# Decode attention with two key heads a unit in one TensorE loop, in place of one key head a unit

## The chip, the cores and the metric

The kernel runs on one core of one Trainium2 chip. The metric is the device time in microseconds of that core. "Before" takes 446.25 us, the median of three runs (446.05 to 446.79). Two numbers: the *time* of an execution, which is the metric, and its *span*, which is what the trace covers, from the first to the last instruction.

## The reference, cut to what matters

Two attention layers, A and B, decode one token for each of 4 batches. They differ in what they read of the key and value caches: A reads all 8192 positions, B the last 2048.

```python
B, Sq, D = 4, 1, 512
Hq, Hkv, Sk, Dh = 32, 8, 8192, 128              # rep = Hq // Hkv = 4
q = (x @ wq).reshape(B, Sq, Hq, Dh).transpose(0, 2, 1, 3)
k = repeat(k_cache, rep, axis=1)                # B: only [:, :, Sk - 2048:, :]
v = repeat(v_cache, rep, axis=1)
p = softmax(einsum("bhqd,bhkd->bhqk", q, k) * Dh ** -0.5)
o = einsum("bhqk,bhkd->bhqd", p, v)
y = o.transpose(0, 2, 1, 3).reshape(B, Sq, Hq * Dh) @ wo
# output: concatenate([y_A, y_B], axis=-1)      everything bf16
```

The kernel has to read 184.56 MB from HBM. A's two caches are 134 MB of it, B's 34 MB, the four weight matrices 17 MB.

## The kernel before: the parts that matter

The work is cut into 40 *units*. A unit of A is one key head of one batch: 2 MB of K and 2 MB of V, 128 partitions with 64 positions (16 KB) each. A unit of B is four heads. K and V have four slots each. For every unit TensorE transposes K (T), multiplies it with the queries to get the scores (S), and multiplies the exponentials of the scores with V (PV). DVE finds the maximum and subtracts it, ACT takes exp, DVE and POOL add up the probabilities. After all batches of a head, its outputs are multiplied with that head's rows of wo.

The order of the instructions of one unit on TensorE, and which unit's values it carries:

```python
TOKENS = [("T", 0), ("T", 1), ("OT",), ("T", 2), ("T", 3), ("S", 0), ("S", 1), ("X",),
          ("T", 4), ("T", 5), ("S", 2), ("S", 3), ("PV", 0), ("PV", 1), ("OL",),
          ("T", 6), ("T", 7), ("S", 4), ("S", 5), ("PV", 2), ("PV", 3), ("S", 6), ("S", 7), ("OPJ",)]

def pv_unit(u):                      # L is the last unit
    if u < L - 1:
        return u - 1
    return None if u == L - 1 else L - 2
```

The end is treated specially. The last K is loaded directly after the K before it, ahead of two V, and no values stand between the last K and its scores except those of unit L-2. The values of the last two units come after the scores of the last one, and the last V arrives in quarters. `pe_filler` issues matmuls whose results nobody uses, to keep TensorE busy between the quarters:

```python
add(dve_sub(L)); add(dve_sum(L)); add(dve_rcp(L))
add(act_exp(L))
add(pool_ar2(L))
for c in range(NQ):
    pe_PV(L - 1, c)
add(dve_norm(L - 1))
for c in range(NQ):
    pe_PV(L, c)
    if c < NQ - 1:
        pe_filler(2)
add(dve_norm(L))
pe_OPJ(L // Bn)
# ... (queue of loads, on SyncE)
for u in range(1, NU + 1):
    if u < L:
        sp_K(u)
        if u == L - 1:
            sp_K(L)                  # the last K, right after the one before it
    # ... then V of unit u - 1
# after the last V: the last 0.5 MB of wo in four pieces, then the stores
```

Of the kernel before, what the change touches and what calls it, by code (L numbers as in the profile page):

```python
# [6 lines left out]
BF16 = mybir.dt.bfloat16  # L7
# [7 lines left out]
def bass_concat_heads__gqa_block_cached__sliding_block_cached__decode_kernel(  # L15
# [21 lines left out]
    DC = D // 128  # L37
    NT = SK // 128
    SB = SK // W
    NQ = 4  # L40
    assert SB == 4 and HKV % SB == 0 and NT % 32 == 0 and REP == 4
    TQ = NT // NQ
    NB = NT // 8
    NCMAX = SB * REP
    assert NT * 2 * REP <= 512 and NCMAX <= 16 and Bn <= 8
# [4 lines left out]
    NKS, NVS, NKT, NPT = 4, 4, 4, 4  # L50
    NW = 64
    NR = 4
# [6 lines left out]
    units = []  # L59
    for gg in range(HKV // SB):  # L60
        for b in range(Bn):
            units.append(dict(P=1, b=b, S=2, J=NT // 2, CPT=2 * REP, hq0=gg * SB * REP, nhq=SB * REP, g0=gg * SB, gg=gg))
    NU_B = len(units)
    for g in range(HKV):
        for b in range(Bn):
            units.append(dict(P=0, b=b, S=1, J=NT, CPT=REP, hq0=g * REP, nhq=REP, g0=g))
    NU = len(units)
    L = NU - 1
    NG = NU // Bn
    NG_B = NU_B // Bn  # L70
    LB0, NLB = NU_B + 2, 4
    LB1 = LB0 + (L - 1 - LB0) // NLB * NLB
    assert NLB == Bn and NKS == NVS == NPT == NLB
    first_group = {1: 0, 0: NG_B}
    last_group = {1: NG_B - 1, 0: NG - 1}

    def kv_src(cache, u, q=None):
        un = units[u]
        if un["P"] == 0:
            ap = cache[un["b"], un["g0"]].rearrange("(p t) d -> p t d", p=128)  # L80
            return ap if q is None else ap[:, q * TQ:(q + 1) * TQ, :]
        base = cache[un["b"], un["g0"] + 2 * q, SK - W:SK, :]
        JB = NT // 2
        return bass.AP(tensor=base.tensor, offset=base.offset,
                       ap=[[JB * DH, 64], [SK * DH, 2], [1, JB * DH]])

    def kv_dst(buf, slot, u, q=None):
        un = units[u]
        if un["P"] == 1:
            JB = NT // 2  # L90
            return buf[:, slot, q * JB:(q + 1) * JB, :]
        if q is not None:
            return buf[:, slot, q * TQ:(q + 1) * TQ, :]
        return buf[:, slot, :, :]

    with ExitStack() as es:
# [5 lines left out]
        def ps(name):  # L102
            return es.enter_context(nc.psum_tensor(name, [128, 512], F32))
# [4 lines left out]
        K_sb = sb("K_sb", [128, NKS, NT, DH], BF16)  # L108
        V_sb = sb("V_sb", [128, NVS, NT, DH], BF16)
        KT_sb = sb("KT_sb", [128, NKT, 8 * 128], BF16)  # L110
        W1 = sb("W1", [128, HQ * D], BF16)
        W2 = sb("W2", [128, HQ * D // 2], BF16)
# [3 lines left out]
        NGQ = HQ // REP  # L116
        NGG = HKV // SB
        RQA = sb("RQA", [128, Bn, NGQ, 2, 2 * REP], BF16)
        RQB = sb("RQB", [128, Bn, NGG, 2, 2, 4 * REP], BF16)
        RQc = sb("RQc", [128, Bn, 2, 2 * REP], BF16)  # L120
        zt = sb("zt", [128, Bn], BF16)
        permE = sb("permE", [128, 2, 2, 64], BF16)
        MK = sb("MK", [128, 16], F32)
        MASKB = sb("MASKB", [128, 16], F32)
        M1m = sb("M1m", [128, 16], F32)
        MBm = sb("MBm", [128, 16], F32)
        x_sb = sb("xo_sb", [Bn, 2, D], BF16)
        xT = sb("xT", [128, 2, DC, Bn], BF16)
        QT = sb("QT", [128, 2, Bn, HQ], BF16)
        M1 = sb("M1", [128, 16], F32)  # L130
        MB = sb("MB", [128, 16], F32)
        L1 = sb("L1", [128, 16], F32)
        LB = sb("LB", [128, 16], F32)
        RL = sb("RL", [128, 4, 16], F32)
        Dt = sb("Dt", [128, NT * 2 * REP], F32)
        PT = sb("PT", [128, NPT, NT * 2 * REP + NW], BF16)

        def pt_cols(u, c0, n):
            return PT[:, u % NPT, c0:c0 + n]
        OTg = sb("OTg", [128, 16, Bn], BF16)  # L140
        ORx = sb("ORx", [64, REP, REP, 32], BF16)
        OL = sb("OL", [128, SB, REP, Bn], BF16)
        osb = x_sb
        oacc = sb("oacc", [Bn, D], F32)
        dummy = sb("dummy_t", [128, 2], F32)
        banks_f = [ps("ps%d" % i) for i in range(8)]
        sem_k = [sm("s_k%d" % i) for i in range(NKS)]
        sem_v = [sm("s_v%d" % i) for i in range(NVS)]
        sem_vl = [sm("s_vl%d" % i) for i in range(NQ)]
        sem_wl = [sm("s_wl%d" % i) for i in range(REP)]  # L150
        sem_x = [sm("s_x0"), sm("s_x1")]
        sem_w1 = [sm("s_w1_%d" % i) for i in range(NQP)]
        s_w2 = sm("s_w2")
        sem_out = [sm("s_out0"), sm("s_out1"), sm("s_out2")]
        s_T, s_S, s_PV, s_OPJ = sm("s_T"), sm("s_S"), sm("s_PV"), sm("s_OPJ")
        s_Ed, s_Ea = sm("s_Ed"), sm("s_Ea")
        s_max, s_sub, s_sum, s_rcp = sm("s_max"), sm("s_sub"), sm("s_sum"), sm("s_rcp")
        s_ocp, s_exp, s_otr = sm("s_ocp"), sm("s_exp"), sm("s_otr")
        s_ar1, s_ar2, s_setup = sm("s_ar1"), sm("s_ar2"), sm("s_setup")
        s_pm, s_pm2, s_mk = sm("s_pm"), sm("s_pm2"), sm("s_mk")  # L160
        s_acp = sm("s_acp")
        s_Eq, s_rq, s_opc = sm("s_Eq"), sm("s_rq"), sm("s_opc")
        s_mk0, s_perm = sm("s_mk0"), sm("s_perm")

        KTB = [0, 1, 2]
        STB = [3, 4]
        OTB = [5, 6]
        OPB = 7

        def bank_f(i):  # L170
            return banks_f[i]

        def bank_bf(i):
            return banks_f[i].bitcast(BF16)

        K_sbf = K_sb.bitcast(F32)
        W1wq = W1[:, :].rearrange("p (c n) -> p c n", c=DC)
        W1wo = W1[:, :].rearrange("p (g r n) -> p g r n", g=HKV, r=REP)
        W2wo = W2[:, :].rearrange("p (g r n) -> p g r n", g=SB, r=REP)

        def wo_of(gi):
            if gi == 0:
                return W2wo, 0
            if gi < NG_B:
                return W1wo, 0
            return W1wo, SB + (1 if gi == NG - 1 else 0)

        def sem_of(key):
            t = key[0]
            if t in ("K", "Kh"):  # L190
                return sem_k[key[1] % NKS]
            if t in ("V", "Vh"):
                return sem_v[key[1] % NVS]
            if t == "VL":
                return sem_vl[key[1]]
            if t == "WL":
                return sem_wl[key[1]]
            if t == "x":
                return sem_x[key[1]]
            if t == "out":  # L200
                return sem_out[key[1]]
            if t == "W1":
                return sem_w1[key[1]]
            if t == "wo":
                return sem_w1[2]
            if t == "pm":
                return s_pm if key[2] == 0 else s_pm2
            if t == "E":
                if jobs[key[1]]["kind"] in ("xT", "QP", "perm"):
                    return s_Eq  # L210
                return s_Ed if evac_eng[key[1]] == "dve" else s_Ea
            return {
                "W2": s_w2, "T": s_T, "S": s_S, "PV": s_PV, "OPJ": s_OPJ,
                "max": s_max, "sub": s_sub, "sum": s_sum, "rcp": s_rcp, "otr": s_otr,
                "ocp": s_ocp, "exp": s_exp, "ar1": s_ar1, "ar2": s_ar2, "setup": s_setup, "pset": s_setup,
                "mk": s_mk, "acp": s_acp, "mk0": s_mk0, "perm": s_perm, "rq": s_rq, "OPJc": s_opc,
            }[t]

        DMA_KEYS = ("K", "Kh", "V", "Vh", "VL", "WL", "x", "out", "W1", "W2", "wo", "mk")

        plan = {e: [] for e in ("sp", "pe", "act", "dve", "pool")}

        turn = [None]

        def op(eng, fn, waits=(), inc=None):
            plan[eng].append(dict(fn=fn, waits=[w for w in waits if w is not None], inc=inc, turn=turn[0]))
# [4 lines left out]
        jobs = []  # L231
        bank_last = {}
        evac_eng = {}
        tjob_idx = {}
        qp_idx = {}
        xt_idx = {}
        perm_idx = {}
        ol_idx = {}
        norm_key = {}
        ot_uses = []  # L240

        def new_job(kind, eng, **kw):
            idx = len(jobs)
            step = 2 if turn[0] is not None and kind in ("OT", "OL") else 1
            bank = (jobs[-1]["bank"] + step) % 3 if jobs else 0
            jobs.append(dict(kind=kind, idx=idx, bank=bank, prev=bank_last.get(bank), **kw))
            bank_last[bank] = idx
            evac_eng[idx] = eng
            return idx

        def bankfree(idx):
            return ("E", jobs[idx]["prev"]) if jobs[idx]["prev"] is not None else None

        def pe_job_xT(P):
            idx = new_job("xT", "dve", P=P)
            xt_idx[P] = idx
            bk = bank_bf(KTB[jobs[idx]["bank"]])

# [760 lines left out]
```

## Time and profile before

| before | value | where it is read |
|---|---|---|
| time, median | 446.25 us | run times |
| span of the profiled execution (its time: 447.8 us) | 446.1 us | page, first line |
| DMA busy | 9 tenths in 38 of 40 slices | page, part 2 |
| sum of packet durations | 440.1 us on each of 16 engines | added up from the trace's packet records |
| last big transfer ends | 440.65 us | packet records, on the time axis of the views |
| from there to the end | 5.4 us | 446.07 - 440.65 |

From the profile page: the span, the busy time of each engine with its share of the span and its instructions, then two rows of the part with 40 slices (busy tenths of the DMA engines, and GB/s), and the count of packets.

```profile
span 446.1 us, 14783 instructions
PE 348.1 (78%) x6789; PEld 317.0 (71%) x6789; DVE 195.2 (44%) x451; ACT 179.0 (40%) x202; POOL 42.0 (9%) x127
...
DMA  8999999999999999999999999999999999999993
GB/s 336 417 407 439 414 421 417 419 420 422 424 424 424 429 422 423 426 426 432 428 428 426 428 432 426 428 424 425 430 429 429 423 426 432 430 425 425 428 415 113
DMA packets 17318, 185.01 MB, mean 415 GB/s; under 512 B 1908, under 2 KB 2440, under 8 KB 4872
```

The DMA engines are the limit from the second slice to the last but one. TensorE has 78% and waits in between. The view of waits says for what (engine, tile, line, what was waited for, then us in total, number of waits, longest):

```profile
PE ps L351 <- DMA K_sb<-in_A_k_cache_dram: 20.2, 16, 2.6
PE ps L417 <- DMA V_sb<-in_A_v_cache_dram: 17.9, 13, 2.0
```

In the view of windows each row is a stretch of time with the busy us of every engine, then granted TensorE clock, DMA share and GB/s:

```profile
120.00:400.00 280.00, 227.24 (x4409) 207.17 (x4405) 121.66 (x281) 117.92 (x135) 25.73 (x82) 0.96 1.01 427
436.00:441.00 5.00, 4.37 (x127) 3.78 (x124) 1.69 (x6) 0.42 (x1) 0.80 (x2) 1.00 0.47 178
441.00:446.10 5.10, 2.40 (x42) 1.62 (x38) 0.91 (x3) 0.00 (x0) 0.00 (x0) 1.00 0.00 1
```

In the middle (120 to 400 us) the DMA engines moved 427 GB/s, at a DMA share of 1.01.

How the kernel ends is seen in the timeline (start, duration, engine, line, operation, operands, count, and in brackets the idle time before it and what ended that):

```profile
436.56 0.42 DVE L524 TENSOR_REDUCE M<-ps 128x4 f32<-128x256 f32 x1 [0.22 <-PE ps L392]
437.45 2.22 PE L417 MATMUL ps<-PT,V_sb 128*128 128x64 bf16 x70 [0.63 <-issue]
437.94 0.42 ACT L573 ACTIVATE PT<-Dt 128x256 bf16<-128x256 f32 x1 [2.08 <-DVE Dt L562]
...
439.94 0.63 PE L417 MATMUL ps<-PT,V_sb 128*128 128x64 bf16 x16
440.84 0.63 PE L417 MATMUL ps<-PT,V_sb 128*128 128x64 bf16 x16
441.74 0.63 PE L417 MATMUL ps<-PT,V_sb 128*128 128x64 bf16 x16
442.67 1.03 PE L493 MATMUL ps<-W,OTg 128*4 128x256 bf16 x8 [0.31 <-DVE OTg L612]
```

Maximum, subtraction and exp of the last unit (436.56 to 438.36) run while TensorE does the values of the unit before (437.45 to 439.67). These 70 matmuls take in the first quarter of the last unit's own values too. When the last bytes are there at 440.65, only the last two quarters, the projection and the store are left.

### The profile page before, as it was taken

How to read it: one execution, taken by the hardware profiler on the slowest of the kernel's cores; microseconds unless marked ns; L12 is line 12 of the kernel's file. 1: busy time of each engine (PE TensorE's matmuls, PEld its weight loads, DVE VectorE, ACT ScalarE, POOL GpSimd, SP SyncE). 2: the span in 40 equal slices, each digit the busy share in tenths (PEclk: the TensorE clock that was granted, in tenths of full speed). 3: DMA queues.
4: the chain of work that ended last, by engine and by line, in shares of the span. 5: the costliest groups of instructions: out<-in, count | busy, mean ns of one | idle time of the engine just before them, and what ended most of it. 6: DMA issues, size and time to landing. Idle time of an engine off the chain costs nothing.

```text
span 446.1 us, 14783 instructions
## 1 busy us (share of the span) xinstructions
PE 348.1 (78%) x6789; PEld 317.0 (71%) x6789; DVE 195.2 (44%) x451; ACT 179.0 (40%) x202; POOL 42.0 (9%) x127
## 2 busy tenths in 40 slices
PE   0585199899685998867978886788879898976997
PEld 0585199868571997866867776778778887866895
DVE  0264055656440645534434543455334344434362
ACT  1063045535430653534433433445334343444261
POOL 3100001000100101001100010001000000100010
PEclk9998579999988999999999999999889998999899
DMA  8999999999999999999999999999999999999993
GB/s 336 417 407 439 414 421 417 419 420 422 424 424 424 429 422 423 426 426 432 428 428 426 428 432 426 428 424 425 430 429 429 423 426 432 430 425 425 428 415 113
DMA packets 17318, 185.01 MB, mean 415 GB/s; under 512 B 1908, under 2 KB 2440, under 8 KB 4872
## 3 DMA queue, kind: packets, MB, share of 16 engines
q1 hardware_dynamic: 15672, 178.80, 95.1%
q10 hardware_dynamic: 1552, 5.78, 3.2%
q8 instruction: 22, 0.36, 0.3%
q14 instruction: 8, 0.07, 0.0%
q0 software_dynamic: 64, 0.01, 0.0%
HBM read 184.56 MB, written 0.01 MB: 414 GB/s over the span
## 4 chain that ended last, share of the span: by engine, by line
DMA 57%; PE 32%; issue 4%; ACT 3%; DVE 3%; POOL 1%; DVEq 0%; ACTq 0%; POOLq 0%
DMA K_sb<-in_A_k_cache_dram 44%; PE ps L351 15%; PE ps L417 7%; DMA W<-in_A_wq_dram 7%; DMA W<-in_B_wo_dram 6%; PE ps L392 5%; ACT KT_sb L360 3%; PE ps L502 2%; PE ps L283 1%; DVE KT_sb L359 1%; DVE M L524 1%; DVE Dt L562 1%; ACT PT L573 1%; POOL PT L630 0%; PE ps L458 0%
## 5 line engine op out<-in xcount | busy, mean ns | idle before, releaser
L360 ACT ACTIVATE KT_sb<-ps 128x1024 bf16<-128x1024 bf16 x160 | 162.5, 1023 | 240.7 <-PE ps L351 237.8
L351 PE MATMUL ps<-identf,K_sb 128*128 128x128 f32 x1280 | 182.8, 290 | 36.9 <-DMA K_sb<-in_A_k_cache_dram 20.2
L351 PEld LDWEIGHTS ps<-identf,K_sb 128*128 128x128 f32 x1280 | 146.5, 147 | 50.8 <-DMA K_sb<-in_A_k_cache_dram 21.8
L359 DVE COPY KT_sb<-ps 128x512 int32<-128x512 int32 x160 | 110.2, 689 | 133.9 <-PE ps L351 133.1
L417 PE MATMUL ps<-PT,V_sb 128*128 128x64 bf16 x2560 | 90.0, 195 | 19.7 <-DMA V_sb<-in_A_v_cache_dram 17.9
L417 PEld LDWEIGHTS ps<-PT,V_sb 128*128 128x128 bf16 x2560 | 81.7, 99 | 21.9 <-DMA V_sb<-in_A_v_cache_dram 19.2
L392 PE MATMUL ps<-RQc,KT_sb 128*128 128x32 bf16 x2048 | 76.3, 177 | 1.1 <-ACT KT_sb L360 0.7
L392 PEld LDWEIGHTS ps<-RQc,KT_sb 128*128 128x128 bf16 x2048 | 71.9, 97 | 4.1 <-ACT KT_sb L360 0.9
L594 POOL PARTITION_ALL_REDUCE LB<-L x40 | 17.3, 433 | 138.8 <-DVE L L585 138.8
L533 POOL PARTITION_ALL_REDUCE MB<-M x32 | 11.9, 371 | 184.0 <-DVE M L524 184.0
L612 DVE TENSOR_TENSOR OTg<-ps,RL 128x4 bf16<-128x4 f32 (+1 forms) x40 | 7.0, 174 | 43.9 <-PE ps L417 43.9
L585 DVE TENSOR_REDUCE L<-PT 128x4 f32<-128x256 bf16 (+1 forms) x40 | 22.0, 550 | 5.2 <-ACT PT L573 4.5
L524 DVE TENSOR_REDUCE M<-ps 128x4 f32<-128x256 f32 (+1 forms) x40 | 19.1, 478 | 10.7 <-PE ps L392 10.7
L573 ACT ACTIVATE PT<-Dt 128x256 bf16<-128x256 f32 (+1 forms) x40 | 18.1, 453 | 4.7 <-DVE Dt L562 4.5
L392 PE MATMUL ps<-RQB,KT_sb 128*128 128x16 bf16 x512 | 18.5, 170 | 1.6 <-issue 0.8
L392 PEld LDWEIGHTS ps<-RQB,KT_sb 128*128 128x128 bf16 x512 | 17.8, 98 | 2.5 <-issue 1.0
L502 PE MATMUL ps<-W,OL 128*4 128x512 bf16 x60 | 15.7, 405 | 3.6 <-DMA W<-in_B_wo_dram 3.6
L283 PE MATMUL ps<-xT,W 128*128 128x4 bf16 x256 | 7.4, 165 | 12.0 <-DMA W<-in_A_wq_dram 11.6
L283 PEld LDWEIGHTS ps<-xT,W 128*128 128x128 bf16 x256 | 7.0, 101 | 12.1 <-DMA W<-in_A_wq_dram 11.7
L562 DVE TENSOR_TENSOR Dt<-ps,MB 128x256 f32<-128x256 f32 x32 | 13.3, 415 | 0.5 <-POOL MB L533 0.5
L262 PE MATMUL ps<-ident,xo_sb 4*128 4x4 bf16 x8 | 0.6, 170 | 15.4 <-POOL identf L639 15.4
L502 PEld LDWEIGHTS ps<-W,OL 128*4 128x4 bf16 x60 | 4.6, 88 | 10.6 <-DMA W<-in_B_wo_dram 3.7
(52 smaller groups left out, 67.0 us busy)
## 6 DMA issues: line engine op xcount, KB each, us to landing
K_sb<-in_A_k_cache_dram SPq DMA_DIRECT2D x32, 2048.0 KB, 33.2
V_sb<-in_A_v_cache_dram SPq DMA_DIRECT2D x31, 2048.0 KB, 37.0
K_sb<-in_B_k_cache_dram SPq DMA_DIRECT2D x16, 1024.0 KB, 28.0
V_sb<-in_B_v_cache_dram SPq DMA_DIRECT2D x16, 1024.0 KB, 28.2
W<-in_B_wq_dram SPq DMA_DIRECT2D x1, 4096.0 KB, 12.5
W<-in_A_wq_dram SPq DMA_DIRECT2D x1, 4096.0 KB, 30.2
W<-in_A_wo_dram ACTq DMA_DIRECT2D x7, 512.0 KB, 10.2
W<-in_B_wo_dram SPq DMA_DIRECT2D x1, 2048.0 KB, 29.3
```

The costliest lines, as they stand in the source:

```text
L283: ins = pe.matmul(out=bk[:, hl * Bn:(hl + 1) * Bn], lhsT=W1wq[:, c, hq * DH:(hq + 1) * DH], rhs=xT[:, P, c, :], start=(c == 0), stop=(c == ...
L351: ins = pe.transpose(out=bkf[:, pi * 128:(pi + 1) * 128], in_=K_sbf[:, slot, t0:t0 + 2, :].rearrange("p t d -> p (t d)"), identity=identf[ ...
L359: return e.tensor_copy(out=KT_sb.bitcast(I32)[:, tj % NKT, :], in_=bkf.bitcast(I32)[:, :])
L360: return e.activation(out=KT_sb[:, tj % NKT, :], in_=bk[:, :], func=ACTF.Copy)
L392: ins = pe.matmul(out=dst, lhsT=ktv[:, pi, :, e], rhs=rhs, start=(e == 0), stop=(e == 1))
L417: ins = pe.matmul(out=otb[:, s * NW:(s + 1) * NW], lhsT=V_sb[:, vs, t, :], rhs=pt_cols(u, t * CPT, NW), start=(j == 0), stop=(j == J - 1))
L502: ins = pe.matmul(out=opb[0:Bn, 0:D], lhsT=OL[:, i // REP, i % REP, :], rhs=wo_view[:, wg + i // REP, i % REP, :], start=(P == 1 and first ...
L524: return dve.tensor_reduce(out=M1[:, 0:NC].rearrange("p (s h) -> p s h", h=CPT), in_=stb[:, 0:NT * CPT].rearrange("p (s j h) -> p s h j", ...
L562: return dve.tensor_tensor(out=Dt[:, 0:NT * CPT].rearrange("p (s j h) -> p s j h", s=S, h=CPT), in0=stb[:, 0:NT * CPT].rearrange("p (s j h ...
L573: return act.activation(out=PT[:, u % NPT, 0:NW], in_=Dt[:, 0:NW], func=ACTF.Exp, scale=scale)
L585: return dve.tensor_reduce(out=L1[:, 0:NC].rearrange("p (s h) -> p s h", h=CPT), in_=PT[:, u % NPT, 0:NT * CPT].rearrange("p (s j h) -> p ...
L594: return pool.partition_all_reduce(LB[:, 0:NC], L1[:, 0:NC], channels=128, reduce_op=ReduceOp.add)
```

## The change

The intent: read A in rows of 32 KB instead of 16, with half as many transfers; run one small TensorE loop for the whole kernel, so that fewer instructions have to be fetched (the instruction queue q8 moved 22 packets before; page, part 3); and take the sums of the probabilities from DVE and POOL to TensorE. A unit is now two heads of A or eight of B, 4 MB of K and 4 MB of V, 20 units, two slots each. Two units are one turn of the loop, ten turns. The diff is a rewrite of most of the file; this is its core.

```diff
-NKS, NVS, NKT, NPT = 4, 4, 4, 4
-    for gg in range(HKV // SB): ...            # B: 8 units of four heads
-    for g in range(HKV):
-        for b in range(Bn):
-            units.append(dict(P=0, b=b, S=1, J=NT, CPT=REP, ...))     # A: one head
+    units = [dict(P=1, b=b) for b in range(Bn)]                       # B: eight heads
+    units += [dict(P=0, b=b, gp=gp) for gp in range(NSEG) for b in range(Bn)]  # A: two heads
# ... K_sb and V_sb have two slots of 4 MB; a mask of -1e30 keeps the two heads apart
-        TOKENS = [("T", 0), ("T", 1), ("OT",), ...]
-        def pv_unit(u): ...
+        LA = 3
+        for k in range(NJ + LA):               # NJ = 16 transposes of 4
+            if k < NJ:
+                TOK.append(("T", k))
+            if k >= LA:
+                TOK.append(("S", k - LA))
+            if k == PV0 - 1:                   # PV0 = 10
+                TOK.append(("SM",))            # sums of unit u - 1, on TensorE
+            if k >= PV0 and pc < NC:
+                TOK.append(("PV", pc))         # values of unit u - 1
+                pc += 1
+        AFTER = {("S", 2): ("OT",), ("S", 5): ("OL",), ("S", 8): ("OPJ",)}   # in odd units
         for u in range(NU):
+            turn[0] = tn = u // 2              # every unit is in the loop
# ... after the loop
-        for c in range(NQ):
-            pe_PV(L - 1, c)
-        for c in range(NQ):
-            pe_PV(L, c)
-            if c < NQ - 1:
-                pe_filler(2)
+        op("pe", pe_seed, waits=[("ocp", NTURN - 1)])
+        pe_SM(L)
+        for c in range(NC):
+            pe_PV(L, c, bank=KTB[0], waits=[("VL", vch_of[c])])
# ... loads
         for u in range(1, NU + 1):
-            if u < L: sp_K(u); ...             # the last K early
+            if u < NU:
+                kv_load("K", u)
+            kv_load("V", u - 1)
+            if u % 2 == 0 and tn in pieces:
+                op("sp", dma(Wo_sb, ...), inc=("wo", tn))       # 1 MB of wo per turn
+        # after V of the last unit (in pieces of 4, 2, 1, 1 eighths): the last 1 MB of wo
```

So the loads end in this order: K18, V17, 1 MB of wo, K19, V18, V19, 1 MB of wo. Units are counted from 0; L = 19.

## The prediction

> **What bounds it now.** The DMA engines. In the forty slices their busy share is 9 except in the first and last, with 425 to 429 GB/s from 120 to 400 us; the trace's packet records add up to 440.1 us on each of 16 engines, in a span of 446.1. [...] TensorE is busy 348 us (page part 1) but waits only 20.2 us for K and 17.9 us for V of A (view of waits). The chain of waits alternates a 33 us K transfer with 7 us of TensorE: a queue 33 us deep, not a starved one. Last bytes land at about 441.4 us.

> **What the change does.** The same 184.6 MB are read. Rows of A grow from 16 to 32 KB: a packet took 614 ns at 16 KB and 1218 ns at 32 KB (wq). 8064 packets become 4032: 310.4 us per engine become about 307.9 (estimate), -2.5 us. B keeps 8 KB rows (314 ns). Half the completions (1844, 9 ns each): -0.4. Less unrolled TensorE code, so fewer of the 22 instruction packets (1.08 us each): -0.6. The last wo piece has 1 MB in 1 KB rows instead of 0.5 MB: +0.2. Last bytes at about 438 us (estimate).

> TensorE keeps its 1280 transposes, 2560 score and 2560 value matmuls (0.92 us per 8, 0.39 per 16, 0.95 per 32). A new unit takes 7.4+3.1+3.8+0.5 (the new sums) = 14.8 us, an odd one 2 us more for each turn's projection, against 20 us of DMA. DVE loses the sums over PT (22 us): not critical, no gain.

> Two 4 MB slots replace four of 2 MB. K of unit u+1 needs the transposes of u-1, done about 16 us after that unit's K landed; its turn on the engines comes after 28. Some 12 us of slack: no starving.

> **The tail is lengthened.** After the last K come V18, V19 and 1 MB of wo: 22.8 us, so K19 lands at about 415. Unit 19 waits at its first value matmul for V18 (425); then 9.6 us of transposes, scores, values and projection, to 434.6. Then in series: max 0.7; combine, mask, all-reduce, unmask 1.2; two subtractions 1.4; exp of 1024 columns 1.1; sums 0.7; 128 value matmuls 3.8; normalisation 0.6; 16 projection matmuls 2.0; copy and store 2.2: about 448.5. Before, this chain ran on half-size units and hid under the last V.

> **Predicted: 447.5 us, 8 in 10 within 443 to 453.** Faster by over 2%: 0.04; within 2%: 0.87; slower: 0.09.

> **What would show it.** A-packets of about 1.22 us; 430 to 432 GB/s in the middle; DMA busy 9 until about 438; TensorE waiting 2 to 5 us for K and V in nearly every unit; last K landing at 414 to 416; about 10 us from last byte to end, filled by values, exp and projection (before: 5).

> **What would make it wrong.** DMA gaps because a 4 MB slot comes free late. [...] Slow starts: absorbed in the middle, 1 to 3 us in the tail. A shorter tail if the steps overlap better than I add up: 443 to 445. Below 440 the bytes do not allow.

After 434.6 the terms add up to 13.7 us, so to 448.3, which the text gives as about 448.5. The durations of its terms are read off the trace of the kernel before, or scaled up from there: max and subtraction of 512 columns took 0.69 us, exp 0.41 us for 256 columns and 0.63 for 512, 8 projection matmuls 1.03 us, an all-reduce 0.37 us. Its packet records have 314.6 ns for 8 KB, 615.9 for 16 KB (median 614) and a median of 1218 for the 32 KB of wq (mean 1266), 9.2 ns for writes of 8 bytes or less, and 1.07 us for each of the 22 instruction packets. The landings, the last bytes and the sum are estimates from these, and so are the "1 to 3 us" of slow starts.

## The result, and the profile after

| | before | after |
|---|---|---|
| time, median (range), runs | 446.52 us (446.05 to 446.82), 4 | 454.22 us (453.79 to 454.46), 4 |
| span of the profiled execution | 446.1 us | 451.5 us |
| sum of packet durations per DMA engine | 440.1 us | 435.6 us |
| packets | 17318 | 13047 |
| idle time of a DMA engine between 2.5 and 430 us (mean of 16) | 0.01 us | 0.04 us |
| last big transfer ends | 440.65 us | 438.44 us |
| from there to the end of the span | 5.4 us | 13.1 us |

The ratio of the two is 1.0172, with a 95% interval of 1.0155 to 1.0190: the kernel became 1.7% slower, within the 2% that counts as the same. A ratio here is always the mean time of one kernel's fast runs over that of the other's of the same rounds, so it isn't quite the ratio of the medians. A time of 454.22 us is 1.2 us above the predicted range, 443 to 453.

The page of the kernel after:

```profile
span 451.5 us, 15657 instructions
PE 367.6 (81%) x7282; PEld 340.9 (76%) x7282; DVE 207.8 (46%) x473; ACT 182.0 (40%) x183; POOL 21.3 (5%) x56
...
DMA  8999999999999999999999999999999999999950
GB/s 358 406 414 421 420 418 420 422 446 430 422 430 441 427 425 427 436 432 424 430 434 431 427 441 425 427 427 431 437 424 427 437 434 422 433 439 424 409 192 2
DMA packets 13047, 184.78 MB, mean 409 GB/s; under 512 B 1332, under 2 KB 2408, under 8 KB 4456
```

The DMA row is as full as before, and then it ends with a 5 and a 0: for the whole last slice of 11.3 us next to nothing is transferred (2 GB/s). The same in the windows:

```profile
120.00:400.00 280.00, 240.77 (x4704) 224.14 (x4700) 139.84 (x311) 122.54 (x123) 8.42 (x28) 0.93 1.00 429
436.00:441.00 5.00, 1.75 (x30) 0.89 (x26) 2.76 (x8) 1.06 (x1) 0.37 (x1) 0.99 0.03 12
441.00:451.60 10.60, 7.34 (x150) 6.61 (x147) 1.41 (x5) 0.37 (x1) 0.00 (x0) 0.82 0.01 2
```

The middle is a little faster (429 GB/s after 427). From 436 to 441 TensorE is busy for only 1.75 us of 5 (before: 4.37), and after 441 it has 150 matmuls left, at a clock of 0.82. The waits:

```profile
PE KT L257 <- DMA K_sb<-in_A_k_cache_dram: 29.5, 7, 4.5
PE OT L304 <- DMA V_sb<-in_A_v_cache_dram: 3.8, 5, 1.5
```

The two together are 33.3 us (before 38.1), in fewer and longer waits. TensorE still waits for the DMA engines and not the other way round. The end, in the timeline:

```profile
416.64 3.42 PE L257 MATMUL KT<-identf,K_sb 128*128 128x128 f32 x16 [4.42 <-DMA K_sb<-in_A_k_cache_dram]
...
426.51 0.63 PE L304 MATMUL OT<-PT,V_sb 128*128 128x64 bf16 x16
427.72 1.89 PE L367 MATMUL KT<-Wo_sb,OL 128*4 128x512 bf16 x8
...
436.28 0.69 DVE L396 TENSOR_REDUCE M<-SB 128x8 f32<-128x512 f32 x1 [2.63 <-PE SB L290]
438.08 0.69 DVE L434 TENSOR_TENSOR Dt<-SA,MBm 128x512 f32<-128x512 f32 x1
439.40 1.06 ACT L443 ACTIVATE PT<-Dt 128x1024 bf16<-128x1024 f32 x1 [4.28 <-DVE Dt L434]
440.51 0.78 PE L316 MATMUL SA<-PT,onesb 128*128 128x64 bf16 x16 [2.10 <-ACT PT L443]
441.10 5.33 PE L304 MATMUL KT<-PT,V_sb 128*128 128x64 bf16 x128
447.02 0.27 PE L659 MATMUL SA<-Wl_sb,OT_sb 128*4 128x256 bf16 x1 [0.59 <-DVE OT_sb L473]
449.29 0.29 SPq L538 DMA_DIRECT2D out_dram<-osb  x1
```

The last K is there at 416.64. The first values of unit 18 start at 426.51, when V18 has landed (426.32 by the semaphore records, which have the moment at which a transfer's completion is signalled). TensorE was not idle before them: the first half of unit 19's transposes and scores had kept it busy just as long, so the last K and V18 bind within 0.2 us of each other. From there it takes until 436.28 for the maximum of the last scores to start, because these values, one projection and the second half of the last unit's own transposes and scores stand in one row on TensorE. Then maximum, subtraction, exp, sums, values, projection and store follow each other; none of them has anything to hide behind. The DMA engines gained 2.2 us, and the tail lost 7.7 us; that makes 5.4 us between the spans (451.5 - 446.1; the two terms add up to 5.5 by rounding). The rest of the 7.7 us between the medians is that the time of the profiled execution lies 2.3 us above its span (before: 1.7), that the profiled execution of before was a slow one of its kind (447.8 us, with a median of 446.5), and that the one of after was 0.4 us below its median.

### The profile page after: what moved, and what is told of

It is laid out like the page before. It is cut to its first block, busy times and chain, and to the rows that moved or that the text cites. A ratio compares the mean times of both kernels' runs of the same rounds, so it can differ in the third digit from the quotient of the medians.

```text
span 451.5 us, 15657 instructions
## 1 busy us (share of the span) xinstructions
PE 367.6 (81%) x7282; PEld 340.9 (76%) x7282; DVE 207.8 (46%) x473; ACT 182.0 (40%) x183; POOL 21.3 (5%) x56
## 2 busy tenths in 40 slices
DMA packets 13047, 184.78 MB, mean 409 GB/s; under 512 B 1332, under 2 KB 2408, under 8 KB 4456
## 4 chain that ended last, share of the span: by engine, by line
DMA 43%; PE 40%; issue 7%; DVE 5%; ACT 4%; SPq 1%; POOL 0%; POOLq 0%
DMA K_sb<-in_A_k_cache_dram 21%; PE KT L257 18%; DMA V_sb<-in_A_v_cache_dram 15%; PE OT L304 10%; DMA K_sb<-in_B_k_cache_dram 7%; PE SB L290 4%; PE KT L367 3%; PE SA L290 2%; ACT PT L443 2%; DVE Dt L434 2%; ACT KT_sb L266 2%; DVE KT_sb L265 1%; PE SA L316 1%; PE KT L304 1%; DVE M L396 1%
## 5 line engine op out<-in xcount | busy, mean ns | idle before, releaser
L266 ACT ACTIVATE KT_sb<-KT 128x1024 bf16<-128x1024 bf16 x160 | 161.2, 1021 | 231.3 <-PE KT L257 231.0
L257 PE MATMUL KT<-identf,K_sb 128*128 128x128 f32 x1280 | 211.8, 301 | 49.2 <-DMA K_sb<-in_A_k_cache_dram 29.5
L257 PEld LDWEIGHTS KT<-identf,K_sb 128*128 128x128 f32 x1280 | 151.9, 153 | 53.0 <-DMA K_sb<-in_A_k_cache_dram 30.2
L265 DVE COPY KT_sb<-KT 128x512 int32<-128x512 int32 x160 | 110.2, 689 | 126.5 <-PE KT L257 126.0
L304 PE MATMUL OT<-PT,V_sb 128*128 128x64 bf16 x2560 | 100.5, 193 | 3.8 <-DMA V_sb<-in_A_v_cache_dram 3.8
L304 PEld LDWEIGHTS OT<-PT,V_sb 128*128 128x128 bf16 x2560 | 84.3, 97 | 8.9 <-DMA V_sb<-in_A_v_cache_dram 4.4
L290 PEld LDWEIGHTS SA<-RQc,KT_sb 128*128 128x128 bf16 x1280 | 56.7, 99 | 6.8 <-ACT KT_sb L266 3.0
L290 PE MATMUL SA<-RQc,KT_sb 128*128 128x16 bf16 x1280 | 57.0, 171 | 1.1
L290 PE MATMUL SB<-RQc,KT_sb 128*128 128x16 bf16 x1280 | 55.8, 170 | 1.3 <-issue 1.3
L290 PEld LDWEIGHTS SB<-RQc,KT_sb 128*128 128x128 bf16 x1280 | 51.7, 97 | 2.5 <-issue 1.4
```

Source lines behind the costliest of these rows:

```text
L257: ins = pe.transpose(out=bkf[:, pi * 128:(pi + 1) * 128], in_=K_sbf[:, slot, t0:t0 + 2, :].rearrange("p t d -> p (t d)"), identity=identf[ ...
L265: return e.tensor_copy(out=KT_sb.bitcast(I32)[:, tj % NKT, :], in_=bkf.bitcast(I32)[:, :])
L266: return e.activation(out=KT_sb[:, tj % NKT, :], in_=bk[:, :], func=ACTF.Copy)
L290: ins = pe.matmul(out=stb[:, t % NTH * C:(t % NTH + 2) * C], lhsT=ktv[:, pi, :, e], rhs=RQc[:, u % 2, t // TS, e, :], start=(e == 0), stop ...
L304: ins = pe.matmul(out=otb[:, s * NW:(s + 1) * NW], lhsT=V_sb[:, slot, t, :], rhs=PT[:, slot, t * C:t * C + NW], start=(j == 0), stop=(j == ...
```

## The experiments

There were twelve runs, each compared with the kernel before on the same chip and in the same rounds. Runs of the same group share a chip.

| run | what it is | median us (range) | ratio to before [95%] |
|---|---|---|---|
| *group 1* (before 446.01) | | | |
| after_ctl | the kernel after, unchanged | 453.58 (452.73 to 454.87) | 1.0168 [1.0146, 1.0191] |
| e1_wo_late | a wo piece after the last K | 455.14 (454.34 to 456.08) | 1.0201 [1.0180, 1.0222] |
| e2_wl_early | the last wo before the last K | 456.54 (455.79 to 457.05) | 1.0226 [1.0206, 1.0245] |
| e3_filler | TensorE kept busy before the last values | 452.12 (451.58 to 453.80) | 1.0148 [1.0124, 1.0173] |
| *group 2* (before 446.86) | | | |
| e4_rows16 | 16 KB rows again | 456.12 (455.62 to 456.18) | 1.0209 [1.0191, 1.0228] |
| e5_peel | last turn out of the loop, scores of L first | 449.47 (448.87 to 449.90) | 1.0059 [1.0043, 1.0076] |
| e6_peel_wo | e5 and e1 together | 446.17 (445.92 to 446.78) | 0.9992 [0.9975, 1.0009] |
| e7_peel_wo_fill | e6 and fillers before the last K | 446.16 (445.88 to 446.44) | 0.9987 [0.9971, 1.0003] |
| *group 3* (before 446.19) | | | |
| e8_peel_wo_khalf | e6, last K in two halves | 445.83 (445.44 to 446.01) | 0.9983 [0.9968, 0.9997] |
| e9_unroll | last turn out of the loop, order unchanged | 453.35 (453.14 to 455.25) | 1.0156 [1.0137, 1.0175] |
| *group 4* (before 447.02) | | | |
| e10_early_proj | e8, projections one turn earlier | 446.55 (445.53 to 447.43) | 0.9990 [0.9971, 1.0009] |
| e8_again | e8 once more | 445.68 (445.56 to 446.43) | 0.9977 [0.9962, 0.9991] |

In group 4 one run of the kernel before took 606.26 us (its granted clock was 1.0, not lower than in the other runs); its cause is not known, and it is left out of the ratios.

My theory at the start (A): the time came from the serial chain of TensorE, DVE and ACT behind the last loads, which the bigger units made longer; I took the landing of the last K for its beginning. Two rivals: (B) the bytes or the DMA engines set the end, for instance because a 4 MB slot comes free too late; (C) the code of the loop itself is slow on TensorE.

### The control

> The changed kernel once more, as the control of this batch: about 454.2 us, a span of 451 to 452. Both theories expect the same. Its own purpose: how far time and span differ for this kernel and for the one before (2.3 us for this one so far).

Measured: 453.58 us, ratio 1.0168. The result stands.

### e1: a wo piece moved behind the last K

```diff
-            if u % 2 == 0 and tn in pieces: (load of the wo piece, before K19)
+            if u == L: (the last such load, after K19)
```

> Only the order of two loads: the wo piece of the last turn (1 MB) goes after the last K instead of before it. The bytes are the same. Theory A (the end is set by the serial chain that starts when the last K lands): the last K lands about 2.5 us earlier, and the time falls by as much, to about 451.7. Theory B (the end is set by the DMA, by starving in the middle or by the total of bytes): no change, within 0.5 us of the control. Theory C (TensorE is too slow in the middle of the run and arrives late at the last K): no change, for the last unit would start when TensorE is free.

Measured: 455.14 us, 0.3% slower than the control, with intervals that overlap. Two lines of its timeline say why I was wrong:

```profile
414.26 3.35 PE L257 MATMUL KT<-identf,K_sb 128*128 128x128 f32 x16 [1.95 <-DMA K_sb<-in_A_k_cache_dram]
426.53 0.64 PE L304 MATMUL OT<-PT,V_sb 128*128 128x64 bf16 x16 [2.33 <-DMA V_sb<-in_A_v_cache_dram]
```

The last K came 2 us earlier (414.26 after 416.22 in the control), and TensorE then waited 2.33 us for V18, which came no earlier, as nothing that was loaded before it had been taken away. So A fell in its first form, which saw the last K alone as the beginning of the chain. Two things bind: K19, and V18 because its values stand before the last scores. The prediction had this right (it let unit 19 wait for V18), and the experiment's expectation did not.

### e2: the last wo before the last K

```diff
+            if u == L: (load of the last 1 MB of wo, before K19)
-        (the same load, after V19)
```

> The opposite: the 1 MB of wo for the last projection is loaded before the last K instead of at the very end. Same bytes. Theory A: the last K lands about 3 us later (1 KB rows), the time rises by 2.5 to 3.2 us to about 457. Theory B: no change or a gain, since the last bytes are now values, which the kernel waits for anyway. Theory C: no change up to the slack of TensorE.

Measured: 456.54 us, 0.6% slower than the control. The bytes end at 438.3 us, as in the kernel after (438.4), and the end of the span moved from 451.3 to 454.9.

```profile
419.26 3.67 PE L257 MATMUL KT<-identf,K_sb 128*128 128x128 f32 x16 [7.34 <-DMA K_sb<-in_A_k_cache_dram]
```

Last K and V18 came some 3 us later, and so did everything after. The same bytes, done at the same time, with a later end: theory B falls.

### e3: TensorE kept busy before the last values

```diff
         op("pe", pe_seed, waits=[("ocp", NTURN - 1)])
+        pe_filler(12, KTB[1])                  # 12 matmuls that nobody reads
         pe_SM(L)
```

> Twelve matmuls of 512 columns without use (2.6 us) fill the pause of TensorE between the last scores and the last exp, as the kernel before had such fillers in its tail. If the half clock seen at 441.2 to 444.6 us comes from that pause: the 128 last value matmuls take 3.8 us instead of 5.15, the time falls by about 1.3 us. If the clock falls for another reason[...]: no change of the 5.15 us and of the time. If the fillers end later than the exp, up to 0.5 us of it is lost again.

Measured: 452.12 us, 0.2% faster than the control by the ratios, whose intervals overlap. The fillers and the last values in the timeline:

```profile
437.75 2.76 PE L642 MATMUL KT<-RQ,ident 128*128 128x512 bf16 x12
440.82 3.90 PE L304 MATMUL KT<-PT,V_sb 128*128 128x64 bf16 x128
```

And windows (the third number from the end is the granted clock): for the kernel after the stretch before its clock falls, the stretch at half clock and the last values, then the last values in e3:

```profile
437.45:440.86 3.41, 1.31 (x16) 0.54 (x17) 1.66 (x5) 1.06 (x1) 0.37 (x1) 1.00 0.02 7
440.86:444.27 3.41, 3.41 (x70) 3.41 (x67) 0.63 (x2) 0.00 (x0) 0.00 (x0) 0.50 0.02 5
441.10:446.50 5.40, 5.33 (x132) 5.21 (x129) 0.66 (x3) 0.00 (x0) 0.00 (x0) 0.71 0.01 3
```

```profile
440.80:444.80 4.00, 3.92 (x135) 3.79 (x131) 0.67 (x3) 0.00 (x0) 0.00 (x0) 1.00 0.02 4
```

128 value matmuls took 3.90 us at full clock and 5.33 us at 0.71. The half clock cost 1.4 us in the traces; in the five other profiled runs that keep the order of the kernel after and have no fillers (after_ctl, e1, e2, e4, e9) these matmuls took 5.02 to 5.69 us. The medians of control and e3 differ by 1.5 us, but two of the five times of e3 (453.80 both) lie within the control's range, so the times alone would not show it.

### e4: 16 KB rows again

```diff
-            op("sp", dma(buf[:, slot, :, :], src), inc=(kind, u, 0))
+            for hf in range(2):                # each 4 MB load as two of 2 MB
+                t0 = hf * NTH
+                src = bass.AP(..., offset=base.offset + t0 * DH, ap=[[NT * DH, 128], [1, NTH * DH]])
+                op("sp", dma(buf[:, slot, t0:t0 + NTH, :], src), ...)
```

> Each 4 MB load of problem A is issued as two loads with rows of 16 KB, everything else as in the changed kernel. If a packet costs a fixed 10 ns or so on top of its bytes, as the 614 ns and 1218 ns of before say, the sum of the packet times per engine rises by 2 to 3 us (434.1 to about 436.6), the last K lands about 2.3 us later, and the time rises from 453.6 to about 456. If row length has nothing to do with the gain in bytes: no change. (Two loads per slot also let a first half land earlier, but nothing waits for a half.)

Measured: 456.12 us, a ratio of 1.0209 after 1.0172 and 1.0168 of the kernel after. The packet durations add up to 439.1 us on each engine (kernel after: 435.6), the last bytes end at 440.74 (438.44), and the span of the profiled execution is 453.9 (451.5). The 32 KB rows are worth 2.3 us at the last bytes (predicted for them: 2.5) and some 1.8 us by the ratios (0.41% of 446, e4 against the control; the two intervals just touch), and the tail behind them stayed as long as it was: 453.89 - 440.74 = 13.2 us, after 13.1. So the gain of the longer rows was real (e4 also has twice as many transfers of A, which it does not tell apart from the rows), and the tail spent it.

### e5: the last turn out of the loop, with the scores of the last unit first

```diff
-            turn[0] = tn = u // 2
+            tn = u // 2
+            turn[0] = tn if tn < NTURN - 1 else None        # the last turn is unrolled
# ... in the order of TensorE:
+                elif u == L:
+                    pass                        # no SM, no PV among the T and S of unit 19
+            if u == L:
+                pe_SM(L - 1)
+                opj_last = pe_job_OPJ(tn)
+                for c in range(NC):
+                    pe_PV(L - 1, c, waits=[("V", L - 1)] if c == 0 else [])
# ... and DVE normalises unit L - 1 after it has subtracted the maximum of unit L
```

> The last turn is taken out of the loop, and in the last unit the values, sums and projection of the unit before move behind all its transposes and scores, where TensorE otherwise pauses for the softmax. Loads and their order as in the changed kernel. Theory A2 (the tail is a serial chain: last K, then a whole unit in which the scores of the last unit stand in line with the values of the one before and with their V, then softmax, then values): the last scores end 6 us earlier (about 430 instead of 436), the pause of 4 us of TensorE goes, the 128 last value matmuls take 3.8 us instead of 5.3, and the time falls by 5 to 7 us, to about 447.5. Theory B (DMA sets the end; the last bytes land 12.8 us before it, so this is near refuted): no change. Theory C (the last unit is slow because the loop's TensorE code is slow): taking it out of the loop without saving work gains less than 2 us.

Measured: 449.47 us, ratio 1.0059: 1.1 points of the 1.7 are gone, by nothing but another order of the same instructions, on TensorE and with it on DVE (e9 below tells it from the unrolling).

```profile
416.55 3.38 PE L257 MATMUL KT<-identf,K_sb 128*128 128x128 f32 x16 [3.80 <-DMA K_sb<-in_A_k_cache_dram]
...
430.77 0.69 DVE L396 TENSOR_REDUCE M<-SB 128x8 f32<-128x512 f32 x1 [1.46 <-PE SB L290]
...
433.89 1.06 ACT L443 ACTIVATE PT<-Dt 128x1024 bf16<-128x1024 f32 x1 [3.57 <-DVE Dt L434]
...
439.04 3.90 PE L304 MATMUL KT<-PT,V_sb 128*128 128x64 bf16 x128
```

The last maximum starts 5.5 us earlier than in the kernel after (430.77, 436.28), and TensorE does the values of unit 18 while DVE and ACT go from maximum to exp. It stays busy then, and the last values take 3.90 us, as they did at a clock of 1.00 in e3. The last bytes still end at 438.4 us.

### e9: the last turn out of the loop, order unchanged

```diff
-            turn[0] = tn = u // 2
+            tn = u // 2
+            turn[0] = tn if tn < NTURN - 1 else None
```

> Control of the peel: the last turn is taken out of the loop but all its instructions keep their order. Theory A2 (the order in the last unit was what counted): the changed kernel's time, within 1 us (it saves one loop branch of about 1.2 us, which falls in the wait for a K, and adds instruction fetches). Theory C (the loop itself slowed the last turn): most of the 4 us that the peel gained.

Measured: 453.35 us, ratio 1.0156, within the scatter of the kernel after. The last maximum did not move forward (the profiled execution, 455.25 us, was the slowest of the five):

```profile
437.58 0.69 DVE L396 TENSOR_REDUCE M<-SB 128x8 f32<-128x512 f32 x1 [3.21 <-PE SB L290]
```

So it is the order and not the unrolling that e5 gained by; for the last turn theory C falls. (At the loop's branch TensorE paused in the kernel after for 1.25 to 1.34 us, put down to issue, before the first transposes of each turn but the first. That it costs nothing in the middle is seen from the DMA engines, which were idle for 0.04 us between 2.5 and 430 us.)

### e6: both

The edit is that of e5 and that of e1 together.

> As the last, and the wo piece of the last turn goes after the last K, which alone gained nothing (the last K came 2 us earlier, but the values of the unit before it then waited 2.3 us for their V, which comes no earlier). With the values moved behind the scores, A2 expects the 2 us of the earlier K to count now: about 445.5, 1 to 2.5 us below the run with the peel alone. If the V of the last unit binds by then, under 0.7 us.

Measured: 446.17 us, ratio 0.9992: the loss is gone.

```profile
413.55 3.02 PE L257 MATMUL KT<-identf,K_sb 128*128 128x128 f32 x16 [1.81 <-DMA K_sb<-in_A_k_cache_dram]
...
435.25 3.90 PE L304 MATMUL KT<-PT,V_sb 128*128 128x64 bf16 x128
```

The move that was worth nothing in e1 is now worth 0.7 points, because V18 no longer stands before the last scores, and the last K alone starts the chain. The last values begin 3.8 us before those of e5 and 5.9 us before those of the kernel after. A single edit that brings nothing is not yet worthless: it may be hidden behind a second limit.

### e7: fillers before the last K

```diff
+            if u == L:
+                pe_filler(10, ...)             # while TensorE waits for the last K
```

> As the last, and ten useless matmuls of 512 columns keep TensorE busy while it waits for the last K, so that the first 16 transposes run at full clock (1.9 us instead of 3.4). A2 expects up to 1.5 us less than without, about 444.5, which would be below the kernel before (446.0). If the V or the last bytes of wo bind by then: no change.

Measured: 446.16 us, ratio 0.9987, the same as e6.

```profile
414.84 1.91 PE L257 MATMUL KT<-identf,K_sb 128*128 128x128 f32 x16
```

The first 16 transposes took 1.91 us after 3.02 (in e6 the clock was 0.63 from 413.4 to 416.8), but began 1.3 us later (414.84 after 413.55): in this execution the last K landed 0.6 us later (414.08 after 413.50 by the semaphore records), and the fillers held them up for the other 0.8 us. Gain and loss cancel. Fillers ahead of a load whose landing is not known to the microsecond are a gamble.

### e8 and its repetition: the last K in two halves

```diff
+            if kind == "K" and u == L:
+                for hf in range(2):            # halves with their own semaphores
+                    op("sp", dma(buf[:, slot, t0:t0 + NTH, :], src), inc=(kind, u, 0) if hf else ("KL", 0))
+                return
```

> The run with the peel and the late wo piece, and the last K comes as two loads of half the columns, each with its own semaphore, so that the first eight blocks of transposes of the last unit need only the first half, which lands 4.9 us earlier than the second. TensorE had waited 1.8 us for the whole K there and then run the first transposes at half clock (3.0 us instead of 1.9). Theory A2: the last unit starts as soon as the unit before it is done, at full clock: 2 to 3 us less, about 443.5, below the kernel before. If the last V or the last bytes of wo (438.2 us in the trace) bind by then: 0 to 1 us less.

> The run with the half K loads once more, as the control on the same chip: ratio to the kernel before 0.997 to 1.000.

Measured: 445.83 and 445.68 us, ratios 0.9983 [0.9968, 0.9997] and 0.9977 [0.9962, 0.9991]. This is the fastest version, by 0.2%, of both kernels; I had expected about 443.5 us and got a few tenths of a microsecond off e6. The trace of the second run shows what the rest went into:

```profile
433.68 2.73 PE L304 MATMUL KT<-PT,V_sb 128*128 128x64 bf16 x88
437.49 1.34 PE L304 MATMUL KT<-PT,V_sb 128*128 128x64 bf16 x40 [1.07 <-issue]
```

The last values now start 1.6 us before those of e6 (433.68, 435.25), stop in the middle for 1.07 us, and end only 0.3 us earlier. They do not stop for the last V: its last piece had landed at 435.90 by the semaphore records, and a piece ends after 64, 96 or 112 matmuls, not after 88. The trace puts the pause down to issue, which is what it says when it finds no semaphore event for a wait. What stands beside it in the packet records is a 16 KB packet of the queue that carries the program's instructions, from 435.02 to 436.13. Pauses put down to issue among the values of the last units are also in other traces without a loop there: e5 (0.63 us), e6 (0.20), the first run of e8 (0.25), e9 (0.42), e10 (1.81) and the kernel before (0.63, at 437.45). All seven pauses end 1.2 to 1.5 us after the end of a 16 KB packet of that queue. The kernel after moved 8 such packets in its span, e8 14 and the kernel before 22 (page, part 3). So e8 may be limited by instructions that come late, as a price of taking the last turn out of the loop. This is not shown: no run tests it, and the records do not say whose instructions a packet holds. What they do show is that the expectation of e10, which takes the pause for a wait for the last V, is wrong.

### e10: projections a turn earlier

```diff
-    T0P = 3
+    T0P = 2                                    # the wo pieces and their projections, a turn earlier
# ... so that the unrolled last turn has no projection; the rest as in e8
```

> As the run with the half K loads, and each projection is done one turn earlier, so that the last unit has no transposes or projection of its own turn (2.3 us of TensorE work less behind the last K); all wo pieces then come before the last K, which delays it by 2.6 us, but its first half lands before TensorE is free for it. Theory A2: TensorE is what binds behind the last K, the last value matmuls end up to 2 us earlier until the last V binds (it was waited for at 437.5 us, 0.25 us long): 0.5 to 1.5 us less than that run, about 444.8, so about 1.3 us below the kernel before. If the last V binds wholly: no change.

Measured: 446.55 us, ratio 0.9990: no gain. With less work in the last turn TensorE came to the values of unit 18 earlier and then paused for 1.81 us after 121 of the 128, from 430.8, again put down to issue and ending 1.5 us after a packet of the instruction queue (430.01 to 431.11). The clock fell to half from 433.62 to 437.04, which made the last values slow:

```profile
432.58 0.36 PE L304 MATMUL OT<-PT,V_sb 128*128 128x64 bf16 x7 [1.81 <-issue]
434.82 4.90 PE L304 MATMUL KT<-PT,V_sb 128*128 128x64 bf16 x128
```

## Why the prediction was wrong

The mechanism was right: the same bytes, a DMA time that shrinks by 2 to 3 us, no starving of the queue, and a tail that takes it back. What failed is the sum for the tail, and the step from the sum to the predicted number. "About 10 us from last byte to end" were 13.1, because two terms were too small, the wait for V18 and the 128 value matmuls; and a sum on the axis of the span was given out as a time, and rounded down. Point by point:

- **"Last bytes at about 438 us."** Measured 438.44; 32 KB packets took 1220 ns, 16 KB packets 616 ns (means). The end of the transfers came 2.2 us earlier (440.65 to 438.44); predicted were 3.4 (441.4 to 438), from a start that was put too late. e4 confirms the part of the rows separately.
- **"Some 12 us of slack: no starving."** Right: a DMA engine was idle for 0.04 us in 427 us.
- **"K19 lands at about 415."** The transposes began at 416.64, so 1.6 us late, and the first 16 took 3.42 us (clock 0.55 from 416.6 to 420.1; they took 1.91 in e7).
- **"Unit 19 waits at its first value matmul for V18 (425)."** That V18 can bind is shown by e1; in the kernel after TensorE reached it 0.2 us after it had landed, without a wait. The landing was at 426.32, the start at 426.51: 1.5 us more than in the sum. The 9.6 us from there to the last scores took 9.8.
- **"128 value matmuls 3.8."** This term was mis-sized: 5.33 us in the kernel after. It was taken from a place where TensorE runs at full clock. Here TensorE had almost nothing to do from 436.3 to 440.5, the clock fell to half, and the values paid 1.4 us for it. In the 3.41 us before the fall TensorE was busy for 1.31 us, and its longest pause from 436.3 on was 2.1 us. The prediction names slow starts at its end ("1 to 3 us in the tail") and then left them out of the sum. The trace of the kernel before could have shown it: its clock fell to 0.50 at 40.71 us, in the transposes after a pause of 2.92 us, and at 313.77 us, after 3.41 us in which TensorE was busy for 1.76 us. e3 measured the term without the half clock: 3.90 us.
- **"About 448.5", then "Predicted: 447.5 us".** The sum ends on the axis of the trace, so 448.5 is a span. The measured span is 451.5, and the 3.0 us between are the two items above; the small differences of the other terms (the store took 0.4 us longer, projection and subtractions 0.2 us less each) cancel. But the metric is the time, and it lay 2.3 us above the span in the profiled execution. Before, the profiled execution had a span of 446.1 and the median of the times was 446.25, and I took the two for the same thing. They agree only because that execution was slow: its own time was 447.8, and other executions of the kernel before with times of about 446.0 have spans of 444.3. This cost 2.3 us. Rounding the sum down by 1.0 us, for which the text has no other ground than that the steps might overlap, cost the rest.

So the miss of 6.7 us is made up of 1.5 (V18 late), 1.5 (values at half clock), 2.3 (span taken for time), 1.0 (rounded down) and 0.4 us (the median was above the profiled execution). All of them have the same sign. The range of 443 to 453 was also built around the wrong axis: 448.5 as a span and two microseconds more would have been a time of about 450.5.

The class that the prediction held most likely, within 2%, is the one that came, but with luck: the change was forecast at 1.3 us (446.25 to 447.5) and cost 7.7, which is just under 2%.

That K19 came late is mostly the whole stream: by the semaphore records it landed at 416.60 and the last bytes at 438.87, so 22.3 us lay between where the sum had 22.8, and the end, for which the sum had 438, was 0.9 us late by the same record. Why the stream ended there was not tested. When the clock falls is described by the runs and not explained (next section but one).

## What to carry to other kernels

Where the DMA engines are the limit, bigger units can make the stream a little faster (here 2.2 of 440 us), and they make the work behind the last load longer: count the tail separately, in order of time, before such a change. Take the last turn out of a loop and reorder it: in it, the scores of the last unit should come before the values of the unit before, so that DVE and ACT have their part done while TensorE is busy, and the last K should be loaded ahead of what its chain doesn't wait for; together that was worth 1.8 points here (1.0172 to 0.9992), while the earlier K alone brought nothing. When a prediction is added up on the trace's axis, add the difference between the time and the span of the same execution, and put a half-clock term where the trace shows TensorE with little to do: here it was busy for 1.31 us of 3.41, never idle for longer than 2.1 us, and the clock of 0.50 that followed cost 1.4 us.
